# Attention of the later head pairs on 64x64 quadrants, with interleaved tokens, in a fused hourglass attention and ReGLU kernel

## The chip, the cores and the metric

The kernel runs on one core of a Trainium2 chip. The metric is the device time of one execution in microseconds (us); lower is better. The core has a matrix engine (TensorE, PE in the profile, with its weight loads listed as PEld), VectorE (DVE), ScalarE (ACT), GpSimd (POOL) and SyncE (SP), each with an instruction queue of its own that is worked through in order, and DMA queues that are fed from SP, ACT and POOL.

## The reference

The inputs q, k, v have the shape 8 batches x 8 heads x 576 tokens x 64 dimensions, in fp32. Each head has two attentions whose results are added; the outputs of the heads, laid side by side, are 4608 rows of 512, which go through a gated feed-forward network (FFN).

```python
factor = 4; Sd = S // factor; scale = 1.0 / np.sqrt(D)
q_d = q.reshape(B, H, Sd, factor, D).mean(axis=3)     # and k_d, v_d likewise
out_d = sm_attn(q_d, k_d, v_d)                        # full softmax over 144 pooled tokens
out_up = np.repeat(out_d, factor, axis=2)
mask = np.abs(pos[:, None] - pos[None, :]) < factor   # a band of 7 keys
scores = np.where(mask, scale * q @ k.T, -1e9)
out_local = softmax(scores) @ v
x = (out_up + out_local).transpose(0, 2, 1, 3).reshape(B * S, H * D)
out = (np.maximum(x @ w_gate, 0.0) * (x @ w_val)) @ w_out     # d_ff = 1536
```

## The kernel before

**Pairs and chunks.** The 64 (batch, head) problems are handled as 32 head pairs, numbered 0 to 31, four to a batch; the two heads of a pair take 64 of the 128 partitions each. The attention result of a pair is written in fp16 to `xT` (512 features on partitions, 4608 tokens). The FFN runs in 9 chunks of 512 tokens. From chunk 1 on its three products are done by seven-product (Strassen-like) forms, whose matmuls of 128x256 stand at L1200, L1296 and L1037; plain products are L952. While the FFN of one chunk is computed, the attention of four later pairs is woven in.

**Order.** One long string of steps, `SEQ`, sets the order of instructions by hand; a step names a pair (`a` or `b`), a half and a chunk (`scores/a/1@3`). Each engine keeps the order in which its instructions are emitted. For chunks 2 to 6 the same sequence of 242 to 254 steps repeats. Before them lies a front part with the weight loads and pairs 0 to 11, after them the FFN of the last chunks.

**Pairs 0 to 11** use an older method with smaller tiles, whose lines matter here only as examples: scores on 64-row tiles (L622, L633), outputs on 64-column tiles (L723, L732, L744, L753) or full ones (L780, L788), transposes on PE (L550), the mask on DVE (L649), and for pair 11 a pooling of v on POOL (L574, L587).

**Pairs 12 to 31** (`NEW = 12`) use full 128x128 tiles throughout, with both heads in one matmul:

- q and k are cast to fp16 while they are loaded, four DMAs a pair on POOL's queue (L469), and transposed by a DMA of SP (`emit_qkT`, L530), so that dimensions lie on partitions.
- `emit_pool` (L537) sums groups of four tokens of q and k by one DVE reduction.
- `emit_kk` (L800) and `emit_kd` (L807) copy the keys, on ACT, into block-diagonal operands: 64 keys of head 0 in the upper left, 64 of head 1 in the lower right. The zeros around them are filled in beforehand (`emit_zero`, L814, L822).
- `emit_scores` does four matmuls for the pooled scores (L837) and ten for the near ones (L841), in blocks of 58 queries against 64 keys. ACT takes the exponentials (L850, L855), DVE applies the band mask (`emit_mask_st`, L863).
- `emit_out_st` does the denominators with a matrix of ones (L868, L883) and the numerators with v (L868, L888), all on 128 rows and columns. ACT turns the denominators into reciprocals by Ln and Exp; DVE multiplies (`emit_xn_st`, L903) and adds the pooled part, repeated four times, to the near part (`emit_xsum_st`, L907).
- v comes twice: in blocks for L888 (POOL's queue, L487), and in fp32 for its pooled sums (SP's queue, L521). The sums run on POOL: `emit_v2` (L574) and two of `emit_v1` (L582).

**Fences.** Steps called `after`, `tm` and `tn` are tiny copies into a tile `seen` on POOL (L1466, L1525, L1528). They read a result of another engine, so that a buffer's later load on POOL's queue stands behind it. Output rows are stored by SP (`emit_out`, L987). `next` and `sum` steps are the FFN's operand sums on DVE (L1031, L1176); the gate is L1391, and L1314 finishes products.

Of the kernel before, what the change touches and what calls it, by code (L numbers as in the profile page):

```python
# [27 lines left out]
ex/3/0/0 tu/2/1/4 hv/0/0/7 wv/1 hv/0/1/7 tu/2/0/4 ex/3/1/0 vd/3/6 ma/3/0 ones/6 warm/4/1 const/0 const/1 xp/2/1/5  # L28
vc/3/6 xp/2/0/4 ma/3/1 sd/3/6 xe/2/1V/5 xe/2/0A/4 loadq/6 tr/4/0/0 rd/3/6 su/3/4 td/3/6 tr/4/1/2 loadk/6 ru/3/4
hv/1/0/1 ev/4/11A/2 tu/3/0/4 hg/0/0/6 ev/4/10A/2 hg/0/1/6 tu/3/1/4 loadv/6 tr/4/2/3 ev/4/01A/0 ev/4/00A/0 xp/3/1/5  # L30
ev/4/21V/3 ev/4/20V/3 xp/3/0/4 wg/2 hv/0/2/7 xe/3/1V/5 xe/3/0A/4 hg/1/0/0 s1/4/2 wv/2 hv/0/3/7 ex/4/0/2 hv/1/1/1
loadq/7 hg/1/1/0 hg/1/2/0 ed/4/2 ma/4/0 hv/1/2/1 hg/0/2/6 hg/0/3/6 ex/4/1/2 hg/1/3/0 hv/1/3/1 relu/0/6 tr/5/0/2
ma/4/1 tr/5/1/3 loadk/7 relu/1/0 tr/5/2/4 den/4/1/5 ev/5/20V/4 vd/4/6 ev/5/10A/3 hg/3/*/0 ev/5/21V/4 gate/0/7 vc/4/6
# [5 lines left out]
hg/7/*/1 ed/6/4 relu/7/1 ma/6/0 loadv/8 ev/7/11V/0 hg/8/*/2 relu/8/2 hg/6/*/6 relu/6/6 tr/7/2/3 zs/0.1/0@1  # L39
ev/7/21A/3 qk/a2/0@1 qk/b1/0@0 qk/b0/0@0 den/6/1/5 tr/7/0/0 qk/b2/0@0 ev/7/00A/0 zs/0.0/0@1 qk/b3/0@0 qk/a2/1@0  # L40
ev/7/20A/3 ev/7/01V/0 v/b/0@0 den/6/0/4 ln/4 inv hv/8/*/6 hv/6/*/0 gate/8/6 s1/7/4 tr/8/0/2 gate/6/0 ex/7/0/4
ev/8/00A/2 tr/8/1/1 ev/8/10A/1 zs/1.0/0@1 ev/8/01A/2 ev/8/11A/1 ma/7/0 hv/7/*/3 hg/9/*/0 num/6/0/2 v4/a/0@1 ed/7/4
zero/k/0 gate/7/3 ex/7/1/4 relu/9/0 xsum/5 num/6/1/3 xn/2 tr/8/2/4 hv/9/*/1 ev/8/20A/4 qk/a3/1@0 qk/b3/1@0 ma/7/1
ev/8/21A/4 vd/7/7 v/a/1@0 qk/a0/1@0 qk/a1/1@0 hg/10/*/6 den/7/0/4 flip/9 zs/1.1/0@1 qk/a1/0@1 gate/9/1 qk/a3/0@1
v4/b/1@0 den/7/1/5 qk/a0/0@1 xsum/6 wt/0 hv/10/*/3 vc/7/7 relu/10/6 gate/10/3 ln/4 inv num/7/0/6 num/7/1/7 xn/6
next/0/1@0 hg/11/*/2 xsum/7 relu/11/2 zero/b/6 hv/11/*/1 gate/11/1 scores/a/0@1 exp/a1/0@1 wt/1 sumhi/0/0@1 vd/8/0
vc/8/0 ed/a/0@1 p/1/0@1 next/1/1@0 keep/1/0@1 exp/a0/0@1 zero/b/5 p/2/0@1 flip/10 hg/0/0@1 sumhi/1/0@1 p/6/0@1
mask/a1/0@1 o/a01/0@1 qk/b0/0@1 mask/a0/0@1 o/a00/0@1 o/a11/0@1 c11//0@1 p/5/0@1 o/a10/0@1 qk/b2/1@0 wt/2 keep/2/0@1
p/7/0@1 sum/3/0@1 ln/a0/0@1 hv/0/0@1 relu/0/0@1 hg/2/0@1 wt/3 next/0/0@1 keep/3/0@1 p/4/0@1 c22//0@1 gate/0/0@1
next/1/0@1 ln/a1/0@1 inv/a/0@1 xn/a0/0@1 qk/b1/1@0 relu/2/0@1 qk/b3/0@1 zero/b/1 p/3/0@1 xn/a1/0@1 qk/b0/1@0  # L50
qk/b1/0@1 c21//0@1 flip/12 zero/b/0 qk/b2/0@1 c12//0@1 flip/11 pool/b/0@1 next/2/0@1 xsum/a/0@1 vd/10/1 hg/4/0@1
vc/10/1 v/b/1@0 vd/9/5 vc/9/5 hg/1/0@1 relu/1/0@1 hv/1/0@1 gate/1/0@1 v/a/1@1 scores/b/0@1 exp/b0/0@1 mask/b0/0@1
zs/2.0/0@1 hv/2/0@1 exp/b1/0@1 ed/b/0@1 mask/b1/0@1 gate/2/0@1 hg/3/0@1 pool/a/0@1 hv/3/0@1 relu/4/0@1 relu/3/0@1
gate/3/0@1 o/b01/0@1 o/b00/0@1 v2/a/1@1 o/b10/0@1 o/b11/0@1 ln/b0/0@1 zero/v/0 hv/4/0@1 qk/b0/1@1 gate/4/0@1
hg/5/0@1 v/b/1@1 flip/13 zero/d/0 v2/b/0@1 ln/b1/0@1 v4/b/0@1 p/1/1@1 inv/b/0@1 xn/b1/0@1 relu/5/0@1 keep/1/1@1
xn/b0/0@1 hv/5/0@1 hg/0/1@1 gate/5/0@1 xsum/b/0@1 qk/a1/1@1 v1/a/1@1 zero/b/2 relu/0/1@1 p/6/1@1 next/3/0@1
scores/a/1@1 qk/a0/1@1 p/2/1@1 keep/2/1@1 p/7/1@1 qk/a3/1@1 c11//1@1 p/5/1@1 exp/a0/1@1 mask/a0/1@1 exp/a1/1@1
mask/a1/1@1 ed/a/1@1 o/a00/1@1 o/a10/1@1 keep/3/1@1 o/a01/1@1 kk/a1/1@1 qk/a2/1@1 pool/a/1@1 o/a11/1@1 v1/b/1@1
ln/a1/1@1 qk/b3/1@1 hv/0/1@1 ln/a0/1@1 zs/3.1/0@1 p/4/1@1 qk/b1/1@1 c22//1@1 c21//1@1 pool/b/1@1 inv/a/1@1 kd/a0/1@1
p/3/1@1 c12//1@1 qk/a1/0@2 hg/2/1@1 hg/1/1@1 hv/1/1@1 const/2 kk/a0/1@1 kd/a1/1@1 relu/2/1@1 xn/a0/1@1 v/a/0@1  # L60
qk/a2/0@2 v/b/0@1 xn/a1/1@1 scores/b/1@1 flip/14 relu/1/1@1 exp/b0/1@1 hg/3/1@1 zero/v/1 gate/0/1@1 hv/2/1@1
qk/a0/0@2 exp/b1/1@1 gate/1/1@1 mask/b0/1@1 v2/b/1@1 mask/b1/1@1 zero/d/1 zs/2.1/0@1 gate/2/1@1 ed/b/1@1 v4/b/1@1
zs/3.0/0@1 relu/3/1@1 o/b00/1@1 o/b01/1@1 tn/1/0@1 ln/b0/1@1 o/b11/1@1 o/b10/1@1 ln/b1/1@1 inv/b/1@1 hv/3/1@1
qk/b2/1@1 hg/4/1@1 xsum/a/1@1 v/a/0@2 gate/3/1@1 hv/4/1@1 tn/3/0@1 tm/b/1@1 v4/a/1@1 relu/4/1@1 zero/b/3 xn/b1/1@1
xn/b0/1@1 qk/a3/0@2 v/b/0@2 hg/5/1@1 relu/5/1@1 qk/b1/0@2 zero/b/4 gate/4/1@1 xsum/b/1@1 qk/b2/0@2 hv/5/1@1 zero/k/1
qk/b0/0@2 qk/b3/0@2 gate/5/1@1 zero/v/2 xq/0/0@2 v1/a/0@2 up/2.1/0@2 scores/a/0@2 uk/2.1/0@2 v2/b/0@2 sq/4.0.2.1/0@2
sumhi/0/0@2 exp/a0/0@2 xq/1/0@2 next/0/1@1 xq/3/0@2 sumhi/1/0@2 vh/4.6/0@2 sk/4.0.2.1/0@2 up/2.2/0@2 ed/a/0@2
kk/b1/0@2 sq/4.0.2.5/0@2 sq/4.0.2.6/0@2 xq/2/0@2 vh/10.4/0@2 v2/a/0@2 sk/4.0.2.2/0@2 sk/4.0.2.5/0@2 sum/2/0@2
kk/b0/0@2 next/1/1@1 sq/4.0.2.3/0@2 sq/4.0.2.7/0@2 kk/a0/0@2 sf/4.0.2.22/0@2 mask/a0/0@2 sq/4.0.2.2/0@2 up/2.5/0@2
sq/4.0.2.4/0@2 sf/4.0.2.21/0@2 sf/4.0.2.12/0@2 sum/3/0@2 sf/4.0.2.11/0@2 gt/10.4.3/0@2 up/2.6/0@2 uk/2.2/0@2  # L70
pool/b/0@2 gt/4.6.2/0@2 uk/2.5/0@2 sq/0.0.1.1/0@2 sq/0.0.1.5/0@2 sk/0.0.1.5/0@2 sk/0.0.1.1/0@2 o/a00/0@2 o/a01/0@2
ln/a0/0@2 up/2.3/0@2 sq/0.0.1.6/0@2 sk/0.0.1.2/0@2 up/2.7/0@2 uf/2.22/0@2 o/a11/0@2 kd/b0/0@2 sq/0.0.1.7/0@2
sf/0.0.1.22/0@2 kd/b1/0@2 sq/0.0.1.3/0@2 sf/0.0.1.12/0@2 v1/a/1@2 v1/b/0@2 o/a10/0@2 inv/a/0@2 xn/a0/0@2
scores/b/0@2 sq/0.0.1.4/0@2 sf/0.0.1.21/0@2 up/2.4/0@2 sq/0.0.1.2/0@2 pool/a/0@2 uf/2.21/0@2 sf/0.0.1.11/0@2
sq/1.0.0.1/0@2 sq/1.0.0.5/0@2 vh/6.6/0@2 gt/6.6.2/0@2 sk/1.0.0.1/0@2 sq/1.0.0.6/0@2 uf/2.11/0@2 uf/2.12/0@2
sq/1.0.0.2/0@2 vh/0.2/0@2 ed/b/0@2 exp/b0/0@2 v4/b/0@2 o/b00/0@2 sk/1.0.0.5/0@2 sk/1.0.0.2/0@2 mask/b0/0@2
gt/0.2.1/0@2 sq/1.0.0.3/0@2 sq/1.0.0.7/0@2 sf/1.0.0.22/0@2 o/b01/0@2 kk/a1/0@2 sf/1.0.0.12/0@2 kd/a1/0@2 ln/b0/0@2
next/2/0@2 vh/1.3/0@2 kd/a0/0@2 next/0/0@2 sf/1.0.0.11/0@2 sq/1.0.0.4/0@2 sf/1.0.0.21/0@2 gt/1.3.0/0@2
sq/2.2.0.1/1@2 next/1/0@2 v4/a/0@2 sq/2.2.0.5/1@2 sk/2.2.0.5/1@2 scores/a/1@2 pool/b/1@2 vh/7.1/0@2 sk/2.2.0.1/1@2
qk/a1/1@2 o/b11/0@2 ed/a/1@2 gt/7.1.1/0@2 inv/b/0@2 sq/2.2.0.6/1@2 up/0.1/1@2 up/0.5/1@2 qk/a0/1@2 sk/2.2.0.2/1@2  # L80
sq/2.2.0.3/1@2 sq/2.2.0.7/1@2 exp/a0/1@2 qk/a3/1@2 vh/8.5/1@2 sf/2.2.0.12/1@2 o/b10/0@2 v2/b/1@2 kk/b1/1@2
sf/2.2.0.22/1@2 sq/2.2.0.4/1@2 uk/0.1/1@2 after/3/0@2 next/3/0@2 sf/2.2.0.21/1@2 sq/2.2.0.2/1@2 sf/2.2.0.11/1@2
xsum/a/0@2 mask/a0/1@2 up/0.6/1@2 tm/b/0@2 tm/a/1@2 gt/8.5.1/1@2 kd/b1/1@2 uk/0.2/1@2 v/a/1@2 sq/3.2.1.1/1@2
sk/3.2.1.1/1@2 vh/2.4/1@2 xn/b0/0@2 qk/a2/1@2 sq/3.2.1.6/1@2 sq/3.2.1.2/1@2 qk/a1/0@3 qk/b0/1@2 sq/3.2.1.5/1@2
kk/b0/1@2 gt/2.4.0/1@2 v4/b/1@2 sk/3.2.1.2/1@2 up/0.7/1@2 sk/3.2.1.5/1@2 o/a00/1@2 o/a01/1@2 xsum/b/0@2
sq/3.2.1.3/1@2 sq/3.2.1.7/1@2 o/a10/1@2 kd/b0/1@2 uk/0.5/1@2 uf/0.22/1@2 ln/a0/1@2 qk/b1/1@2 up/0.3/1@2 o/a11/1@2
sf/3.2.1.22/1@2 pool/a/1@2 inv/a/1@2 v2/a/1@2 xn/a0/1@2 sq/3.2.1.4/1@2 sf/3.2.1.21/1@2 v/b/1@2 sf/3.2.1.11/1@2
scores/b/1@2 sf/3.2.1.12/1@2 up/0.2/1@2 ed/b/1@2 up/0.4/1@2 exp/b0/1@2 mask/b0/1@2 tm/b/1@2 sq/5.2.1.1/1@2
sq/5.2.1.5/1@2 kd/a1/1@2 v/a/0@3 v4/a/1@2 v1/b/1@2 o/b00/1@2 o/b01/1@2 uf/0.21/1@2 uf/0.11/1@2 uf/0.12/1@2
sk/5.2.1.5/1@2 vh/3.0/1@2 sk/5.2.1.1/1@2 sq/5.2.1.6/1@2 qk/b2/1@2 xsum/a/1@2 gt/3.0.1/1@2 ln/b0/1@2 vh/9.1/1@2  # L90
gt/9.1.2/1@2 qk/a0/0@3 sk/5.2.1.2/1@2 qk/a2/0@3 sq/5.2.1.2/1@2 sq/5.2.1.7/1@2 kk/a1/1@2 kd/a0/1@2 qk/b1/0@3
sf/5.2.1.22/1@2 qk/b3/1@2 inv/b/1@2 o/b11/1@2 sq/5.2.1.3/1@2 sf/5.2.1.12/1@2 sf/5.2.1.11/1@2 o/b10/1@2 xn/b0/1@2
# [187 lines left out]


def _np_stacked():
    r = np.arange(128)
    i, hh = r % 64, r // 64
    q = np.arange(576)
    band = (i[:, None] - q[None, :] % 58 >= 0) & (i[:, None] - q[None, :] % 58 <= 6)
# [24 lines left out]
def kernel(  # L311
# [29 lines left out]
    B0 = 1  # L341
    WK = 112

    NEW = 12
    QB = 58
    NQB = 10

    cst_dr = nc.inline_tensor(_np_constants(), name="cst").ap()
# [1276 lines left out]
```

## Time and profile before

| | |
|---|---|
| median of 3 runs | 346.62 us (346.43 to 347.88) |
| profiled execution | 346.89 us, span 344.9 us |
| granted TensorE clock | 0.998 |
| PE busy | 330.6 us, 96%, 3410 matmuls |
| DVE busy | 294.7 us, 85%, 578 instructions |
| ACT busy | 270.7 us, 78%, 653 instructions |
| POOL busy | 186.5 us, 54%, 268 instructions |
| DMA | 43.91 MB in 162176 packets, mean 127 GB/s |

The span is the time from the first to the last instruction of the profiled execution; its own time contains about 2 us more around it. A group line of the profile reads: line, engine, operation, output <- inputs with their shapes, count | busy us, mean ns of one | idle time of the engine before them, and what ended it. A timeline line reads: start in us, length in us, engine, line, and so on, with the idle time before it in brackets where there was any. A window line gives, for a stretch of time, its length and each engine's busy time with the number of instructions, the granted clock, the DMA share and GB/s.

### The profile page before, as it was taken

Reading aid. Unit: us, or ns where it says so; the run is one execution under the profiler, and the core shown is the slowest. Engines: PE = TensorE matmul, PEld = TensorE weight load, DVE = VectorE, ACT = ScalarE, POOL = GpSimd, SP = SyncE. Lnnn points to the kernel's source line nnn. Section 1 sums busy time; section 2 is a strip of 40 time slices with the busy share of each in tenths; the row PEclk is TensorE's granted clock in tenths of the full one; section 3 lists DMA queues with packets and bytes.
Section 4 is the critical chain, followed back from the end, with each engine's and each line's share of the span. In section 5 each row is a group of like instructions: output and inputs, shape, how many; then the busy total and the mean of one; then the engine's idle time right before and its main releaser. Section 6 shows DMA issues by size and latency. Waiting matters only on the chain.

```text
span 344.9 us, 9106 instructions
## 1 busy us (share of the span) xinstructions
PE 330.6 (96%) x3410; PEld 243.6 (71%) x3410; DVE 294.7 (85%) x578; ACT 270.7 (78%) x653; POOL 186.5 (54%) x268
## 2 busy tenths in 40 slices
PE   8899999998999999999999999999999999999992
PEld 4764555745558786877687868786868588888881
DVE  6694679999999898979998999899899988886971
ACT  4878798976898898887888888988887558787821
POOL 8994645868988489927993899476040000000000
PEclk9999999999999999999999999999999999999999
DMA  9999999999999999999999999999100200011024
GB/s 138 167 171 209 186 194 165 135 159 205 154 171 156 165 132 190 153 167 104 192 149 175 119 196 115 195 121 174 34 33 2 92 2 31 17 64 46 10 68 138
DMA packets 162176, 43.91 MB, mean 127 GB/s; under 512 B 147500, under 2 KB 156820, under 8 KB 162132
## 3 DMA queue, kind: packets, MB, share of 16 engines
q0 software_dynamic: 123136, 19.51, 81.0%
q1 hardware_dynamic: 38884, 23.80, 31.5%
q8 instruction: 26, 0.43, 0.5%
q14 instruction: 18, 0.15, 0.2%
q10 hardware_dynamic: 112, 0.02, 0.1%
HBM read 46.59 MB, written 9.44 MB: 162 GB/s over the span
## 4 chain that ended last, share of the span: by engine, by line
PE 57%; DMA 18%; POOL 10%; DVE 8%; issue 4%; ACT 1%; SPq 1%; ACTq 0%; POOLq 0%; DVEq 0%
PE ps L1296 20%; PE ps L1200 17%; PE ps L952 13%; DMA v<-in_v_dram 5%; DMA wo_sb<-in_moe_w_out_dram 4%; DMA vw<-in_v_dram 4%; DMA wg_sb<-in_moe_w_gate_dram 3%; POOL qk L469 3%; POOL qk L464 3%; POOL vw L514 2%; DVE gT L1391 2%; PE ps L868 2%; PE ps L883 1%; DMA qk<-in_q_dram 1%; PE ps L888 1%
## 5 line engine op out<-in xcount | busy, mean ns | idle before, releaser
L952 PE MATMUL ps<-xT,wv_sb 128*128 128x512 f16 x352 | 90.4, 379 | 0.0
L952 PEld LDWEIGHTS <-wv_sb 128*128 128x128 f16 x352 | 32.6, 98 | 25.6
L1296 PE MATMUL ps<-xT,qk 128*128 128x256 f16 x240 | 41.0, 272 | 0.3 <-DVE xo L1031 0.3
L1391 DVE SCALAR_TENSOR_TENSOR gT<-r,ps 128x512 f16<-128x512 f16 x55 | 37.3, 681 | 3.0 <-PE ps L952 1.4
L469 POOL DMA_DIRECT2D qk<-in_q_dram x46 | 33.7, 738 | 7.7 <-DMA qkT<-qk 4.8
L469 POOL DMA_DIRECT2D qk<-in_k_dram x46 | 33.8, 738 | 6.9 <-DMA wo_sb<-in_moe_w_out_dram 3.3
L1307 ACT COPY ps<-ps 128x256 f32<-128x256 f32 x80 | 29.2, 370 | 7.8 <-PE ps L1296 5.1
L574 POOL TENSOR_TENSOR v<-v 112x384 f32<-112x384 f32 (+1 forms) x21 | 21.1, 1013 | 20.8 <-DMA v<-in_v_dram 20.3
L1296 PE MATMUL ps<-xT,wg_sb 128*128 128x256 f16 x180 | 31.7, 272 | 0.0
L537 DVE TENSOR_REDUCE qkd<-qkT 128x288 f16<-128x1152 f16 x23 | 30.9, 1343 | 0.3 <-ACT r L1312 0.3
L487 POOL DMA_DIRECT2D vw<-in_v_dram x40 | 29.0, 734 | 1.8 <-issue 1.6
L1296 PEld LDWEIGHTS <-qk 128*128 128x128 f16 x240 | 22.2, 97 | 7.9 <-DVE xT L1283 0.7
L1211 ACT COPY ps<-ps 128x256 f32<-128x256 f32 x54 | 19.4, 372 | 10.1 <-PE ps L1200 9.5
L952 PE MATMUL ps<-xT,wg_sb 128*128 128x512 f16 x104 | 26.4, 379 | 0.2 <-DMA wg_sb<-in_moe_w_gate_dram 0.2
L582 POOL TENSOR_TENSOR vd<-v 48x192 f16<-48x192 f32 x40 | 24.3, 607 | 1.9
L1296 PEld LDWEIGHTS <-xo 128*128 128x128 f16 x240 | 22.9, 98 | 3.0 <-DVE xo L1031 0.3
L1312 ACT CAST r<-ps 128x256 f16<-128x256 f32 x55 | 19.2, 374 | 7.2 <-PE ps L1296 5.9
L1296 PE MATMUL ps<-wt,xo 128*128 128x256 f16 x180 | 24.6, 273 | 0.0
L921 ACT ACTIVATE rden<-rden 128x720 f32<-128x720 f32 x28 | 22.5, 803 | 0.5
L1296 PEld LDWEIGHTS <-wg_sb 128*128 128x128 f16 x180 | 16.4, 97 | 5.3
L1296 PEld LDWEIGHTS <-gT 128*128 128x128 f16 x180 | 17.2, 98 | 3.9
L964 DVE TENSOR_TENSOR gT<-r,ps 128x512 f16<-128x512 f16 x24 | 16.1, 679 | 4.3 <-ACT rden L1577 2.2
(181 smaller groups left out, 885.8 us busy)
## 6 DMA issues: line engine op xcount, KB each, us to landing
out_dram<-y_sb SPq DMA_DIRECT2D x24, 256.0 KB, 4.4
v<-in_v_dram SPq DMA_DIRECT2D x20, 192.0 KB, 5.2
qk<-in_k_dram POOLq DMA_DIRECT2D x46, 72.0 KB, 5.0
qk<-in_q_dram POOLq DMA_DIRECT2D x46, 72.0 KB, 4.8
vw<-in_v_dram POOLq DMA_DIRECT2D x38, 80.0 KB, 5.1
v<-in_v_dram SPq DMA_DIRECT2D x20, 144.0 KB, 5.6
out_dram<-y_sb SPq DMA_DIRECT2D x22, 128.0 KB, 1.8
vw<-in_v_dram POOLq DMA_DIRECT2D x12, 168.0 KB, 7.0
```

The costliest lines, as they stand in the source:

```text
L469: nc.gpsimd.dma_start(dst.rearrange("p (j h d) -> p j h d", h=2, d=64)[:, :, hh, :], _dap(src, off + hh * S * D, [[D, 96], [NQ * D, NB], [ ...
L487: nc.gpsimd.dma_start(t[lo : lo + 64, j0:j1, lo : lo + 64], _dap(v, base + j0 * QB * D, [[D, 64], [QB * D, j1 - j0], [1, D]]),)
L537: nc.vector.tensor_reduce(out=qkd[hp % 2].rearrange("p i t -> p (i t)"), in_=qkT[hp % 4][:, 0 : 2 * S].rearrange("p (t f) -> p t f", f=4), ...
L574: nc.gpsimd.tensor_tensor(out=m, in0=t[:, :, 0:128], in1=t[:, :, 128:256], op=ALU.add)
L582: nc.gpsimd.tensor_tensor(out=vp[hp % 3][lo : lo + 48, :, lo : lo + 64], in0=m[:, :, 0:64], in1=m[:, :, 64:128], op=ALU.add)
L921: nc.scalar.activation(out=rden, in_=rden, func=AF.Exp, scale=-1.0)
L952: nc.tensor.matmul(out=out, lhsT=w[:, kk, bass.ts(jj, 128)], rhs=xT[:, kk, c * TCH : (c + 1) * TCH], start=(kk == 0), stop=(kk == 3),)
L1200: nc.tensor.matmul(out=out, lhsT=self.left[i][t], rhs=self.right[i][t], start=(i == 1 and t == 0), stop=(t == n - 1), skip_group_check=True,)
L1211: nc.scalar.copy(out=o, in_=a)
L1296: nc.tensor.matmul(out=out, lhsT=self.left[i - 1][k], rhs=self.right[i - 1][k], start=(i == 1 and k == 0), stop=(k == n - 1), skip_group_c ...
L1307: nc.scalar.copy(out=o, in_=x)
L1391: lambda c, jj, b, t: nc.vector.scalar_tensor_tensor(out=gT[c % 2][:, jj, :], in0=tg[t], scalar=0.0, in1=ps[:, b, :], op0=ALU.max, op1=ALU ...
```

## The change

For pairs 12 to 31:

- **Tokens interleaved.** q and k are loaded with 12 consecutive tokens on each of 48 partitions (instead of 6 blocks of 96), so after the transpose the 48 columns of one block are the tokens w, w+12, w+24 and so on. Adding four neighbouring tokens becomes two additions of whole contiguous blocks (`emit_pool`).
- **64x64 quadrants.** Nothing is block-diagonal any more. `emit_scores` does 8 matmuls for the pooled scores and 24 for the near ones, in blocks of 48 queries against 56 keys; the head selects the row half of the array, the block's parity the column half. `emit_rows` does the denominators and the numerators: there the parity selects the row half and the head the column half; four matmuls of 112 rows x 64 columns come first in each.
- `emit_kk` becomes two ACT copies over 128 partitions, `emit_kd` and its zero fills go, as do the large fills of `zero/b` and `zero/k`.
- `emit_xn_st` is split in three, two of which write runs of four; `emit_xsum_st` then reads and writes contiguous runs. Except for the last batch in the kernel's order (pairs 28 to 31) the tokens stay in the interleaved order in `xT`, and `emit_out` stores the rows of batches 3 to 6 with a stride of 12: 110 store DMAs instead of 50.
- **v pooled on VectorE.** `emit_v2` and `emit_v1` run on DVE, with one instruction each; the fp32 loads on SP are four a pair instead of two.
- **New order.** The first 273 steps stay, but for one dropped `const`; from there on the order is a new one. The fences go, but for two.

Counted in the two programs: PE matmuls 3410 and 4290, with the FFN's unchanged; DVE 580 and 679 instructions; POOL 273 and 192; DMAs issued by SP 121 and 219.

```diff
-    QB = 58
-    NQB = 10
+    QB = 48
+    NQB = 12
+    KB = 56
...
     def emit_load_q1(hp, i):
+        if hp >= NEW:
+            b, off = head_off(hp)
+            t = qksrc[hp % NS].rearrange("p (i j h d) -> p i j h d", i=2, h=2, d=D)
+            nc.gpsimd.dma_start(
+                t[:, i // 2, :, i % 2, :], _dap((q, k)[i // 2], off + i % 2 * S * D, [[12 * D, 48], [D, 12], [1, D]])
+            )
+            return
...
     def emit_pool(hp):
+        if hp >= NEW:
+            x = qkT[hp % 4][:, 0 : 2 * S].rearrange("p (g h x) -> p g h x", g=6, h=2)
+            nc.vector.tensor_tensor(out=half, in0=x[:, :, 0, :], in1=x[:, :, 1, :], op=ALU.add)
+            h = half.rearrange("p g (f t) -> p g f t", f=2)
+            nc.vector.tensor_tensor(
+                out=qkd[hp % 2].rearrange("p i (w t) -> p (i w) t", w=3), in0=h[:, :, 0, :], in1=h[:, :, 1, :], op=ALU.add
+            )
+            return
...
     def emit_scores(hp, p0):
-        for w, o, a, n in ((0, 0, 0, SD), (2, SD, 0, 72), (1, 798, 0, SD), (2, 798 + SD, 72, 72)):
-            nc.tensor.matmul(
-                out=flat[:, lo + o : lo + o + n], lhsT=kd[r2][:, w, :], rhs=qd[:, a : a + n], start=True, stop=True
-            )
...
+        for jj in range(6):
+            for g in range(2):
+                j = 2 * jj + g
+                for hh in range(2):
+                    r = slice(64 * hh, 64 * hh + 64)
+                    at = lo + 224 + 288 * hh + QB * jj
+                    nc.tensor.matmul(
+                        out=flat[64 * g : 64 * g + 64, at : at + QB],
+                        lhsT=kk[r2][r, KB * j : KB * j + 64],
+                        rhs=qt[r, :, 4 * j : 4 * j + 4],
+                        start=True,
+                        stop=True,
+                    )
...
+    def emit_rows(hp, bank, near, far, wide):
...
+        for g in range(2):
+            for hh in range(2):
+                mm(hh, g, 288, 72, far(slice(0, WK), 0, hh), e[0:WK, hh, 72 * g : 72 * g + 72], stop=False)
+        for g in range(2):
+            for hh in range(2):
+                r = slice(64 * g, 64 * g + 48)
+                mm(hh, g, 288, 72, far(r, 1, hh), e[r, hh, SD:], start=False)
+        for jj in range(1 if wide else 6):
+            for g in range(2):
+                for hh in range(2):
+                    r = slice(64 * g, 64 * g + KB)
+                    if wide:
+                        mm(hh, g, 0, 288, near(r, hh, 0), es[hp % 2][r, 288 * hh : 288 * hh + 288])
+                    else:
+                        mm(hh, g, QB * jj, QB, near(r, hh, jj), x[r, hh, jj])
...
-            nc.gpsimd.tensor_tensor(out=m, in0=t[:, :, 0:128], in1=t[:, :, 128:256], op=ALU.add)
+            (nc.vector if hp >= NEW else nc.gpsimd).tensor_tensor(out=m, in0=t[:, :, 0:128], in1=t[:, :, 128:256], op=ALU.add)
...
+            if NEW // NPB <= b < B - 1:
+                real, step, n = real + 12 * (at % 48) + at // 48, 12, 48 - at % 48
```

## The prediction

> **What bounds the kernel now.** I read the page's engine totals first, then the clock, then busy time by stage, and last the waits and the timeline of TensorE (PE).
>
> ```profile
> PE 330.6 (96%) x3410; PEld 243.6 (71%) x3410; DVE 294.7 (85%) x578; ACT 270.7 (78%) x653; POOL 186.5 (54%) x268
> ```
> ```profile
> core 0: us, PE busy (x) PEld busy (x) DVE busy (x) ACT busy (x) POOL busy (x), PEclk, DMA share, GB/s
> 98.91:133.61 34.70, 34.61 (x346) 26.37 (x344) 32.05 (x61) 31.02 (x74) 25.42 (x39) 1.00 1.48 156
> 133.61:169.16 35.55, 34.77 (x347) 26.47 (x345) 31.59 (x59) 30.32 (x72) 27.08 (x41) 1.00 1.32 153
> 169.16:203.80 34.64, 34.39 (x347) 26.43 (x344) 31.27 (x59) 30.32 (x72) 27.14 (x42) 1.00 1.31 164
> 203.80:238.62 34.82, 34.57 (x349) 26.62 (x347) 31.80 (x59) 30.86 (x73) 27.88 (x41) 1.00 1.44 157
> ```
> Each row is one FFN chunk with the attention of four pairs woven in. PE is busy 97 to 100% of it at a granted clock of 1.00, so PE sets the pace; VectorE (DVE) at 89 to 92% is next. The busy time of PE hides how many waits there are, because a matmul's duration includes its pipeline. In a full stream one matmul starts about N/2.4 + 2 ns after another of N columns (in the records 216 ns at 512, 109 at 256, 62 at 144, 28 at 58). By that rule a chunk takes 33.96 us; the four rows average 34.93. So about 0.97 us per chunk, 3.9 us over the four, is waiting, and between 60 and 99 us another 4.5 us or so.
>
> Three prices come from PE's timeline, early in the run, where tiles smaller than 128x128 occur:
>
> ```profile
> 33.88 0.32 PE L744 MATMUL ps<-att,vw 112*64 112x96 f16 x6
> 34.03 0.23 PE L753 MATMUL ps<-att,vd 72*64 72x72 f16 x4
> 34.10 0.27 PE L550 MATMUL ps<-cst_sb,qk 96*64 96x120 f16 x4
> ...
> 35.66 0.23 PE L753 MATMUL ps<-att,vd 72*64 72x72 f16 x4
> 35.82 0.25 PE L622 MATMUL ps<-qkd 64*72 64x144 f16 x2
> ```
> The same four matmuls of L753 are followed after 0.07 us by a group with the same kind of tile (34.03 to 34.10), and after 0.16 us by one of another kind (35.66 to 35.82). Each change of tile size in the trace costs like this: 90 to 97 ns, 59 times. Second, the four L753 matmuls last 230 ns as a group and 196 ns alone (in the groups), so the last starts 34 ns after the first: two 64-column halves of the array run at once. Third, behind a stall a group with 64-column weights starts its first result 24 ns later than usual, one with 128 columns 12 ns.
>
> The other prices, as groups (busy us, mean ns | idle before):
>
> ```profile
> L537 DVE TENSOR_REDUCE qkd<-qkT 128x288 f16<-128x1152 f16 x23 | 30.9, 1343 | 0.3 <-ACT r L1312 0.3
> L903 DVE TENSOR_TENSOR xn<-ps,rden 128x720 f16<-128x720 f32 x20 | 18.0, 901 | 0.1
> L907 DVE TENSOR_TENSOR xT<-xn 128x576 f16<-128x576 f16 x20 | 16.0, 800 | 0.1
> L863 DVE TENSOR_TENSOR att<-att,zero_sb 128x576 f16<-128x576 f16 x20 | 9.5, 473 | 0.0
> L800 ACT COPY kk<-qkT 64x640 f16<-64x640 f16 x20 | 14.4, 722 | 0.3
> L807 ACT COPY cst_sb<-qkd 64x144 f16<-64x144 f16 x40 | 12.4, 309 | 1.0 <-DVE qkd L537 0.6
> L582 POOL TENSOR_TENSOR vd<-v 48x192 f16<-48x192 f32 x40 | 24.3, 607 | 1.9
> L574 POOL TENSOR_TENSOR v<-v 112x384 f32<-112x384 f32 x20 | 19.9, 1004 | 20.8 <-DMA v<-in_v_dram 20.3
> ```
>
> **PE: fewer columns, more changes of tile.** Per new pair, before: pooled scores 432 columns, near scores 576, pooled outputs 864, near denominator 576, near numerator 576: 3024, or 1260 ns, all on full 128x128 tiles. After: 864+1152 score columns on four quadrants at once count 504; twice (denominator, numerator) 4 far matmuls of 72 at two at a time plus 4 of 72 at four count 432; the near ones 576. That is 1512, or 630 ns, if four quadrants run at once. 20 pairs save 20 x 630 = 12.6 us. Against it: a group of four 48-column matmuls streams in 20 ns, but by the 24 ns weight load plus spacing I take 29; 12 groups in each pair x 20 x 7 ns (some overlap taken off) = +1.7. And the tile changes: scores enter and leave 64x64 (2), each output step goes 128x128, 128x64, 64x64, 128x128 (3 each); counted through the program with the neighbours as ordered, changes rise from 59 to 186: 127 x 94 ns = +11.9. The drop in separate groups gives some 0.6 back: **PE +0.4 us**. Bounds: -1.3 without the weight-load term, +12.6 more if quadrants run only two at a time. All of this lies on the path. I take four at a time, since row halves (L622/L633) and column halves (L744/L753) each run side by side in the trace; no row shows both at once.
>
> **DVE.** Before, per pair: 1343+901+473+800 = 3517 ns. After: two fp16 sums, 576 like L863 (473) and 288 between the 576 and the 128-wide rows (300); mask 473; xn in three, 2 x 452 and 302, scaled from the 256-wide PSUM read (L1314, 419); token sum with contiguous runs 473 (800 still in the last four pairs); v sums of 512 fp32 like L1391 (681) and of 256 like L1314 (419). Sum 4025. Five more instructions per pair overlap their neighbours by 75 to 82 ns each, so +0.1 us a pair; with the last four pairs about +4 us over the run. The zero fills of DVE (1 us) go, and so do 3.9 us in which DVE waited at L1031 for a POOL copy that served as a fence. I cost DVE's work at nothing for PE, covered by its 8 to 11% of idle time; without this cover, at most +4.
>
> **The collisions.** POOL's v sums stretch DVE instructions that run beside them:
>
> ```profile
> 72.73 2.06 DVE L649 TENSOR_TENSOR att<-att,cst_sb 112x576 f16<-112x576 f16 x1
> 73.44 1.04 POOL L574 TENSOR_TENSOR v<-v 112x384 f32<-112x384 f32 x1
> 74.86 0.30 PE L780 MATMUL ps<-att,vw 112*128 112x96 f16 x3 [0.80 <-DVE att L649]
> ```
> The mask of L649 has a median of 451 ns; here it took 2060 and PE stood 0.80 us. Ten DVE instructions are stretched, 6.6 us in all, eight beside POOL's v sums. New pairs' v sums leave POOL, so those near 74, 87 and 240 us go, which held PE for 0.97, 0.5 and 0.44: **-1.9 us**. Those of pair 11 (82, 84 us) stay.
>
> **ACT, POOL, queues.** ACT loses 2 x 723 + 2 x 309 = 2064 ns a pair and gains two copies of 128 partitions (estimated 939 from the 640- and 144-wide rows): -22 us; fills, 7.8 us, shrink to about 2. POOL loses 44 us of sums and the 5 us of fence copies, so its q, k and v loads stand behind nothing but their own buffers. SyncE goes from 121 to 219 DMAs: v loads 40 to 80, and output stores 50 to 110 because batches 3 to 6 leave in rows 12 apart; a store takes 0.43 us to issue, +26 us on a queue that also holds the transposes. I cost that at nothing: spread over 180 us it is 15% of SyncE. If a transpose lands late by more than its lead of three pairs, it is paid in full.
>
> **Sum.** With ACT freed by 1.1 us a pair and DVE free of fences, I take a quarter of the 3.9 us of ordinary chunk waits as gone, -1.0 (0 to -3.9). The new order's other moves I put at zero, between -2 and one more wait per chunk (+5). Profiled execution 346.89 us (span 344.9 and 2.0 around it): 346.9 + 0.4 - 1.9 - 1.0 = 344.4; it stands 0.3 above the median 346.62, so **344.1**. A measurement of this kernel can tell about 0.5%, 1.7 us.
>
> **Rivals.**
> *The quadrants take turns (slower).* If the weight loads of the two row halves cannot run together, a group of four takes 2 x 24 = 48 ns whatever its columns: 12 groups x 19 ns and 7 groups of 72 x 16 ns = 340 ns a pair, +6.8 us, 351; if the streams themselves go two at a time, +12.6, 357. It decides once a four-group of 48 columns takes over 35 ns. For it: four loads per 20 ns of stream is four times what any row shows. Against: the pairs in L753 keep a 34 ns spacing with two loads of 64 in it. The Trainium skill, "TensorE: Matmul & The Clock Gate", section LDWEIGHTS, puts a load at columns/1.2, 53 ns for 64 columns, and by that the sum would be some 8 us higher still; the 34 ns spacing speaks against that figure, but no run here shows four loads at once.
> *DVE's queue stops for a v load (slower).* POOL waited 20.3 us in 4 stretches at L574 for these loads, about 5 us each, and nobody minded; now the same wait blocks the evictions PE needs. The collision shows the cover: 1.6 us of stretch cost PE 0.8. One 5 us wait costs PE 4.3; two of them, 352.7. Against: the new order issues the loads earlier than the 5.6 us that one takes to land.
> *The order is tighter (slower).* One more 1 us wait per chunk: 349.
> *More waits vanish (faster).* If the chunk waits mostly go, another -2.2: about 342.
> *The change does nothing to time*: PE stays the bound with the same stream, and only the collisions' 1.9 us move; that is inside my main case.
>
> **Chances.** Main case 0.47 (341.5 to 348; of it 0.31 under 344.9, 0.13 within the bound, 0.03 above), more waits vanish 0.13, turns 0.15, v load 0.12, tighter order 0.13 (0.03 of it within the bound). Faster 0.44, same 0.16, slower 0.40. The range 340.5 to 353.5 leaves out half of the turns case, a third of the v-load case and a third of the fastest, under 0.2. The likeliest case's own range is 341.5 to 348.
>
> **What would show it.** PE's records: near-score groups spaced 29 ns per four if the quadrants run at once, 48 or more if not; 94 ns at each change of tile; PE's chunk stream about 34.0 us as before. No DVE instruction beside a POOL sum over twice its median after 100 us; DVE idle before its v sums near zero (the v-load rival: microseconds, released by DMA). ACT near 245 us, POOL near 135. I am wrong if attention on PE costs over 35 us for the 20 new pairs, or if DVE's idle time in a chunk is ended by DMA.

## The result, and the profile after

The changed kernel takes 383.06 us (median of 3 runs, 381.09 to 383.56) against 346.62: a ratio of 1.1026 (95% interval 1.0953 to 1.1098), 36 us slower, where 344.1 was forecast in a range to 353.5. Its profiled execution has a span of 381.8 us.

The engine totals, and two chunks of the steady part (columns as before: length, busy us of PE, PEld, DVE, ACT, POOL, granted clock, DMA share, GB/s):

```profile
PE 340.5 (89%) x4290; PEld 237.7 (62%) x4290; DVE 302.6 (79%) x677; ACT 284.5 (75%) x599; POOL 136.4 (36%) x187
```
```profile
141.80:182.50 40.70, 35.65 (x532) 24.73 (x520) 32.37 (x79) 33.67 (x65) 17.06 (x24) 1.00 1.62 146
182.50:223.30 40.80, 35.76 (x540) 24.85 (x525) 32.47 (x79) 33.78 (x65) 18.30 (x26) 1.00 1.27 136
```

A chunk takes 40.75 us instead of 34.6 to 35.6, at the same clock. PE is no longer full (88%), DVE is at 80%, and ACT has gone up to 33.7 us a chunk, though it was to lose 4.4 us. From the scores of pair 12 to those of pair 31 it is 200.5 us against 166.8 (33.7 more), and the stretch after that is 81.9 against 79.1. POOL came out at 136 us as forecast; ACT was forecast at 245 and took 284.5. The groups of ACT, and the largest group of PE's FFN products, say why (busy us, mean ns | idle before; the last line is the same PE group in the kernel before):

```profile
L824 ACT COPY att<-qkT 128x576 f16<-128x576 f16 x10 | 26.8, 2685 | 0.0
L824 ACT COPY kk<-qkT 128x576 f16<-128x576 f16 x10 | 26.8, 2678 | 0.6 <-DMA qkT<-qk 0.6
L829 ACT COPY kk<-qkT 128x96 f16<-128x96 f16 x10 | 3.4, 344 | 0.0
L1340 PE MATMUL ps<-xT,qk 128*128 128x256 f16 x240 | 42.5, 276 | 15.6 <-ACT ps L1351 14.8 <-DVE xo L1074 0.8
```
```profile
L1296 PE MATMUL ps<-xT,qk 128*128 128x256 f16 x240 | 41.0, 272 | 0.3 <-DVE xo L1031 0.3
```

L824 is the large key copy of `emit_kk`. It takes 2.68 us, where the prediction had 0.67 (its 939 ns for both copies, less 0.27 for the small one). PE's idle time ahead of this group went from 0.3 to 15.6 us, nearly all of it ended by ACT's copies at L1351. These move a partial product of PE aside, so that PE can go on in its place; below they are called evictions. The timeline shows such a wait behind one copy, and a different chain behind another:

```profile
188.19 2.68 ACT L824 COPY att<-qkT 128x576 f16<-128x576 f16 x1
...
190.39 0.75 ACT L1351 COPY ps<-ps 128x256 f32<-128x256 f32 x1
...
191.19 0.38 PE L1340 MATMUL ps<-xT,qk 128*128 128x256 f16 x2 [1.56 <-ACT ps L1351]
```
```profile
220.31 2.67 ACT L824 COPY kk<-qkT 128x576 f16<-128x576 f16 x1
...
222.51 0.68 ACT L1356 CAST r<-ps 128x256 f16<-128x256 f32 x1
...
223.04 0.38 PE L865 MATMUL ps<-qkT,kk 64*64 64x48 f16 x24 [0.87 <-ACT kk L824]
...
223.23 0.69 DVE L1435 SCALAR_TENSOR_TENSOR gT<-r,ps 128x512 f16<-128x512 f16 x1 [1.08 <-ACT r L1356]
```

In the first, the eviction stands in ACT's queue behind the copy, and PE waits 1.56 us for it. In the second, the scores wait for the keys, the cast L1356 stands behind the copy, and the gate on DVE waits for the cast. Four such copies a chunk make about 6 us (40.75 against 34.8 without them, in e2 below).

The second surprise is the token sum (durations are min/median/max):

```profile
L945 DVE TENSOR_TENSOR xT<-xn x20: 448/452/2730, 122.4 to 309.2; 128x576 f16<-128x576 f16 x20
```

Sixteen take 0.45 us (forecast 0.47). The four of the last batch, which write in the natural token order, take 2.73 us, not 0.8.

What the two slow instructions share is in the diff: they write single fp16 elements 12 elements, that is 24 bytes, apart (`[12, 4]` as the last step of L824's output; `p (t w f) -> p w f t` in L945). Per element both cost the same: 2685/576 = 4.66 ns and 2730/576 = 4.74 ns.

### The profile page after: what moved, and what is told of

Same layout as the page of the kernel before. It is cut to its first block, busy times and chain, and to the rows that moved or that the text cites. A ratio compares the mean times of both kernels' runs of the same rounds, so it can differ in the third digit from the quotient of the medians.

```text
span 381.8 us, 10880 instructions
## 1 busy us (share of the span) xinstructions
PE 340.5 (89%) x4290; PEld 237.7 (62%) x4290; DVE 302.6 (79%) x677; ACT 284.5 (75%) x599; POOL 136.4 (36%) x187
## 3 DMA queue, kind: packets, MB, share of 16 engines
q0 software_dynamic: 128256, 19.69, 79.1%
q1 hardware_dynamic: 45636, 24.74, 34.8%
## 4 chain that ended last, share of the span: by engine, by line
PE 52%; ACT 18%; DMA 15%; DVE 8%; issue 5%; POOL 1%; DVEq 0%; POOLq 0%; ACTq 0%
PE ps L1340 19%; PE ps L1243 15%; PE ps L990 9%; ACT kk L824 6%; ACT att L824 5%; PE ps L894 4%; DMA vw<-in_v_dram 4%; DMA qk<-in_q_dram 3%; DMA wo_sb<-in_moe_w_out_dram 3%; DMA qkT<-qk 3%; DMA v<-in_v_dram 2%; DVE xT L945 2%; DVE gT L1435 1%; ACT ps L1351 1%; PE ps L865 1%
## 5 line engine op out<-in xcount | busy, mean ns | idle before, releaser
L1340 PE MATMUL ps<-xT,qk 128*128 128x256 f16 x240 | 42.5, 276 | 15.6 <-ACT ps L1351 14.8
L498 POOL DMA_DIRECT2D vw<-in_v_dram x40 | 31.8, 807 | 41.8 <-PE ps L894 26.8
L1351 ACT COPY ps<-ps 128x256 f32<-128x256 f32 x80 | 30.7, 394 | 14.4 <-PE ps L1340 12.3
L1435 DVE SCALAR_TENSOR_TENSOR gT<-r,ps 128x512 f16<-128x512 f16 x45 | 30.7, 690 | 7.6 <-ACT r L1356 4.3
L1340 PE MATMUL ps<-xT,wg_sb 128*128 128x256 f16 x180 | 34.8, 276 | 1.8 <-DVE r L1358 1.3
L824 ACT COPY kk<-qkT 128x576 f16<-128x576 f16 x10 | 26.8, 2678 | 0.6 <-DMA qkT<-qk 0.6
L824 ACT COPY att<-qkT 128x576 f16<-128x576 f16 x10 | 26.8, 2685 | 0.0
L935 DVE TENSOR_TENSOR xn<-ps,rden 128x288 f16<-128x288 f32 x40 | 17.7, 454 | 11.3 <-PE ps L894 10.0
L465 POOL DMA_DIRECT2D qk<-in_k_dram x20 | 13.6, 679 | 29.5 <-DMA qkT<-qk 25.8
L1356 ACT CAST r<-ps 128x256 f16<-128x256 f32 x45 | 17.6, 405 | 7.6 <-PE ps L1340 7.1
L1358 DVE TENSOR_TENSOR y_sb<-ps,q 128x256 f32<-128x256 f32 x20 | 8.4, 421 | 12.7 <-ACT y_sb L1356 9.5
```

The source lines that it names most:

```text
L498: nc.gpsimd.dma_start(t[lo : lo + KB, j0:j1], _dap(v, base + j0 * 2 * QB * D, [[D, KB], [2 * QB * D, j1 - j0], [1, D]]))
L824: nc.scalar.copy(out=_sap(o, (0, 128), 4, [[KB, NQB], [1, 12], [12, 4]]), in_=_sap(x, (0, 128), S, [[4, NQB], [48, 12], [1, 4]]),)
L935: nc.vector.tensor_tensor(out=xn_st[:, 0:S].rearrange("p (a j g b) -> p g j a b", a=12, g=2, b=4)[:, i], in0=ps[:, 6 + i, 0:288].rearrange ...
L1340: nc.tensor.matmul(out=out, lhsT=self.left[i - 1][k], rhs=self.right[i - 1][k], start=(i == 1 and k == 0), stop=(k == n - 1), skip_group_c ...
L1351: nc.scalar.copy(out=o, in_=x)
L1356: nc.scalar.copy(out=o, in_=self.d if i == 11 else self.a)
```

## The experiments

Theory W: these spaced writes cost the time, on ACT by standing ahead of the evictions. Rival Q: the quadrants, their tile changes and the many small matmuls. Rival O: the new order. Theory V came up later: DVE's queue stands behind the loads of pooled v. Every time is set against runs of the kernel before on the same chip.

**e1_runs_out.** The key copy walks in another order, with the same result.

```diff
-                out=_sap(o, (0, 128), 4, [[KB, NQB], [1, 12], [12, 4]]),
-                in_=_sap(x, (0, 128), S, [[4, NQB], [48, 12], [1, 4]]),
+                out=_sap(o, (0, 128), 4, [[KB, NQB], [12, 4], [1, 12]]),
+                in_=_sap(x, (0, 128), S, [[4, NQB], [1, 4], [48, 12]]),
```

> The changed kernel with the first key copy of emit_kk (L824) walked in another order: it writes runs of 12 neighbouring keys and reads elements 96 bytes apart, instead of writing elements 24 bytes apart and reading runs of 4. Same elements, same result. Theory W (the spread-out write makes this copy 2.68 us long and blocks ACT's evictions behind it): the copy falls to 0.6 to 0.8 us, a chunk from 40.75 to about 34.7 us, the time to about 348 us (345 to 352). If reads 96 bytes apart cost the same as writes 24 bytes apart: copy 2.7 us and 383 us again. Rival Q (quadrants, changes of tile and the number of small matmuls cost the time): 375 us or more whatever the copy takes. Rival O (the new order is what is slow): likewise 375 or more.

Measured: 360.67 us, ratio 1.0422 (1.0383 to 1.0461), some 22 us less than the changed kernel but above the 345 to 352 expected. The copy fell only to 1.48 us, not to 0.6 to 0.8: reads 96 bytes apart cost 2.56 ns per element, less than spaced writes, but not nothing. A steady chunk takes 36.4 us.

```profile
L824 ACT COPY kk<-qkT 128x576 f16<-128x576 f16 x10 | 14.8, 1475 | 0.0
```

**e2_flat.** The same copy contiguous on both sides.

```diff
+                out=_sap(o, (0, 128), 4, [[KB, NQB], [1, 48]]),
+                in_=_sap(x, (0, 128), S, [[48, NQB], [1, 48]]),
```

> The changed kernel with the first key copy contiguous on both sides, which leaves the keys in the interleaved order (the band then covers other keys: this part of the computation is changed). It is the floor of this copy's price. Theory W: copy about 0.6 us, time 345 to 350 us, within 2 us of the version that writes runs of 12. Rivals Q and O: 375 us or more.

```profile
L824 ACT COPY kk<-qkT 128x576 f16<-128x576 f16 x10 | 6.7, 674 | 1.0 <-DMA qkT<-qk 1.0
```

Measured: 357.16 us, ratio 1.032 (1.0274 to 1.0367). The copy has the forecast price, 0.67 us, and the undisturbed chunks take 34.8 us. One access pattern accounts for some 25 us: the changed kernel stands 36.4 us over the kernel before of its own series, this one 11.4 (357.16 - 345.72). PE's waits for L1351 have nearly gone (0.8 us). An undisturbed chunk is 0.2 us longer than the shortest of the prediction's four rows (34.64), so little is left for rivals Q and O. The time missed the expected 345 to 350, because earlier chunks now take up to 40.6 us. There a new wait shows, which the slow pace had hidden (next).

```profile
151.82 0.69 DVE L600 TENSOR_TENSOR v<-v 112x512 f32<-112x512 f32 x1 [2.75 <-DMA v<-in_v_dram]
...
153.16 1.64 PE L990 MATMUL ps<-xT,wv_sb 128*128 128x512 f16 x4 [2.29 <-DVE gT L1435]
```

DVE stood 2.75 us for a v load before the first sum of pooled v, and PE 2.29 us for the gate behind it. In the changed kernel itself DVE never waited at L600.

**e3_before_slow.** The kernel before, with one of its two key copies writing elements 32 bytes apart, and nothing else of the change.

```diff
-            out=kk[hp % 2][lo : lo + 64, :, lo : lo + 64],
-            in_=_sap(qkT[hp % 4], (lo, 64), S - 3, [[QB, NQB], [1, 64]]),
+            out=kk[...].rearrange("p j (a b) -> p j b a", b=16),              # second head only
+            in_=_sap(qkT[hp % 4], (lo, 64), S - 3, [[QB, NQB], [4, 16], [1, 4]]),
```

> The kernel before, with the key copy of the second head alone written with elements 32 bytes apart (its 64 keys land in another order within a block: this part of the computation is changed; number of elements, partitions and everything else as before). Theory W: this copy goes from 0.72 to about 3.0 us (640 elements at 4.65 ns), ACT gets 45 us more work, and the time rises from 346.6 to 370 to 390 us though nothing else of the change is there. Rivals Q and O: a slow copy on ACT is hidden, 347 to 350 us.

```profile
L800 ACT COPY kk<-qkT x20: 719/1827/2955, 83.2 to 278.2; 64x640 f16<-64x640 f16 x20
```

Measured: 380.39 us, ratio 1.0983 (1.0949 to 1.1018). The second head's copy takes 2.96 us (4.6 ns per element, on 64 partitions as on 128), the steady chunk 42.1 us. The slow copy alone makes the old kernel almost as slow as the changed one, and PE waits in the same place, for the eviction that is L1351 in the changed kernel (14.8 us there) and L1307 here (us in total, times, longest):

```profile
PE ps L1296 <- ACT ps L1307: 15.9, 10, 1.9
```

Q and O are not needed for the bulk of the loss.

**e4_both.** e1, and the last batch's token sums write contiguously and read 96 bytes apart.

```diff
+            out=x.rearrange("p (w f t) -> p w f t", ...) if b < B - 1 else x.rearrange("p (t w f) -> p t w f", ...),
+            in0=xn_st[:, 0:S].rearrange("p (w f t) -> p w f t" if b < B - 1 else "p (w f t) -> p t w f", ...),
```

> As the version with runs of 12 in the key copy, and besides the token sum L945 of the last four pairs writes contiguously and reads elements 96 bytes apart (same result); before, these four wrote elements 24 bytes apart and took 2.73 us against 0.45 for the other sixteen. Theory W, on VectorE too: these four fall to 0.45 to 0.9 us and the time to 2 to 8 us under the version with the key copy alone, about 343 us. If VectorE's reads with stride cost as much, no difference.

```profile
L945 DVE TENSOR_TENSOR xT<-xn x20: 449/452/1428, 117.1 to 281.8; 128x576 f16<-128x576 f16 x20
```

Measured: 355.56 us, ratio 1.027, 5.1 us under e1. The four sums went from 2.77 to 1.43 us each (5.4 us together): nearly all of it is on the path; 3.5 us of it come behind the last pair's scores (82.0 to 78.5 us from there to the end). Two expectations were missed: the sums did not reach 0.45 to 0.9 us, since reads 96 bytes apart have a price too, and the time is not near 343.

**e5_knat and e7_knat_x.** Same result with no spaced write at all: k is loaded in natural order and the key blocks are one contiguous copy.

```diff
-  [[12 * D, 48], [D, 12], [1, D]]
+  [[D, 48], [48 * D, 12], [1, D]] if i // 2 else [[12 * D, 48], [D, 12], [1, D]]      # loads of k
+  out=_sap(kk[hp % 2], (0, 128), 0, [[KB, NQB], [1, KB]]),                            # emit_kk, one copy
+  in_=_sap(qkT[hp % 4], (0, 128), S - 4, [[48, NQB], [1, KB]]),
```

> The changed kernel with all writes 24 bytes apart designed out, same result: k is loaded in natural order (48 consecutive tokens across partitions), so one contiguous copy of 128x672 makes the key blocks and the second key copy goes; k's pooled sums then read every second element (DVE, four sums of 288 and 144 instead of two of 576 and 288); pooled v rows are loaded in natural order too; and the last batch keeps the interleaved token order up to its output stores, so all twenty token sums L945 write contiguous runs (0.45 us), with 12 more strided output rows groups in the tail. Theory W: key copy about 0.75 us, steady chunk 34.8 us as with the flat copy, time 357 less 4 to 5 us of token sums = 352 to 354. What then stays above 346 is of another kind: theory V says it is waits of VectorE's queue for the pooled-v loads in the first chunks (2.75 us at 149 us in the flat run).

> As the first, but the last batch is put back into natural order by the token sum reading 96 bytes apart (1.43 us each for four sums) and its output is stored in whole rows. If the strided stores of the last batch cost time in the tail, this is faster than the first by 1 to 3 us; if they are hidden, it is slower by up to 2 us (4 sums x 1 us on VectorE).

Measured: e5 357.49 us, ratio 1.031 (1.029 to 1.0331); e7 352.32 us, ratio 1.0156 (1.0133 to 1.0179). The copy takes 0.75 us and ACT 244.4 us in all (247.6 in e2, which has the two copies of the prediction's 245). e5 loses its gain in the tail: from the last pair's scores to the end 84.4 us, against 78.2 in e7 and 79.1 before. The last batch's rows, stored 12 apart, are not hidden there: e5 is 5.2 us over e7, where 1 to 3 was expected. With the effects of e2 and e4, 36.4 - 25.0 - 5.1 = 6.3 us over the kernel before would remain; e7 has 5.6. So the two causes add up, as closely as a run can show that also changed the pooled sums and the loads. In e7's waits of DVE:

```profile
DVE v L606 <- DMA v<-in_v_dram: 7.0, 3, 2.7
```

From one pair's scores to those four pairs later it is 34.9 us in e7 where no such wait falls, and 2.5, 2.7 and 2.5 us more in the three stretches with one. That is 7.6 of the 8.7 us by which e7 takes longer than the kernel before between the scores of pairs 12 and 31 (its front and tail are 1.9 us shorter). So the trace puts what is left on these waits; the runs from e8 on try to take them away.

**e6_vpool.** e5 with the v sums back on POOL (`nc.gpsimd` in `emit_v2` and `emit_v1`).

> The same with the pooled-v sums on POOL as in the kernel before (same result). Theory V: VectorE no longer stands behind a v load, the chunks between 97 and 195 us lose 3 to 6 us, and the time is 346 to 350 us. Rival C (collisions of POOL's sums with VectorE, as in the kernel before at 73 us): steady chunks grow by 0.3 to 1 us each and it comes out the same or slower, 352 to 357.

```profile
130.67 2.53 DVE L887 TENSOR_TENSOR att<-att,zero_sb 128x576 f16<-128x576 f16 x1
...
131.58 1.29 POOL L606 TENSOR_TENSOR v<-v 112x512 f32<-112x512 f32 x1
...
133.25 0.32 PE L894 MATMUL ps<-att,ones_sb 56*64 56x288 f16 x4 [0.87 <-DVE att L887]
```

Measured: 361.69 us, ratio 1.0439 (1.0387 to 1.0491), 4.2 us over e5: rival C's outcome, and slower than its 352 to 357. The mask, 0.46 us alone, takes 2.53 beside a POOL sum. Moving the sums to DVE does take the collisions away, and by these two runs the wait for the loads is the smaller evil.

**e8_vlead and e9_tiles.** A first try at an earlier load went too far.

> The changed kernel with k in natural order and the token sums without 24-byte writes (352.3 us), and in the order only three kinds of steps moved per chunk so that pooled-v loads land before VectorE reaches their sum: v4/b/1 about 46 steps earlier (right behind scores/a/0 of the next chunk), v2/a/1 with v1/b/1 about 22 steps later (right ahead of scores/b/1), v2/b/0 about 16 steps later. Theory V (VectorE's queue stands behind these loads: 1.82, 2.67 and 2.47 us of idle time in the run before, each followed by a chunk 2.5 us longer): those three waits go or shrink under 1 us, time 346 to 349 us. If the waits were only where a general lag shows up: still 351 to 353.

> The same as e8_vlead, and the four far matmuls of 112 rows x 64 columns of each output step replaced by two passes over 64x64 quadrants with as many streamed columns (each half of the array then adds its own pooled keys twice and leaves out the other half's: this part of the computation is changed). It takes away one of three changes of tile size per output step, 8 in a chunk. If a change costs 94 ns of the path, as the prediction had it: a steady chunk shrinks by 0.75 us (34.9 to about 34.1), the time by 3 to 4 us. If changes of tile are hidden: no difference over 1 us.

Measured: 391.47 and 391.13 us. The step `v4/b/1` came to lie ahead of the sum that still had to read its buffer, so that sum took the later pair's v (this part of the computation is changed), and had to wait for it:

```profile
DVE vd L609 <- DMA v<-in_v_dram: 37.0, 5, 10.2
```

That is 30 us more of such waits than in e7, and the run is 39 us longer: a wait in DVE's queue reached the end in full and more, since PE's granted clock also fell (0.956 over the run, 0.999 in e7). The question of the tile changes drowned in it.

**e10_v4early and e11_tiles.** The load steps moved only as far as their buffers allow.

> As e7_knat_x (352.3 us; k natural, no write 24 bytes apart, result unchanged), with three of the four pooled-v load steps per chunk moved up to right behind the sum v1 that frees their buffer (21 to 41 steps earlier); nothing else moves. This is what the run with loads ahead of that sum was meant to be: there each sum stood up to 10 us behind the wrong load. Theory V: the waits of VectorE for v loads (7.0 us in 3) fall under 2 us, the three slow stretches of the run before go, and the time is 346 to 349 us. If what holds the loads is not the order but SyncE's queue (stores of 12-row strides and transposes ahead of them): waits stay, 351 to 353 us.

> The same as e10_v4early, and the four far matmuls of 112 rows x 64 columns of each output step replaced by two passes over 64x64 quadrants with as many streamed columns (each half of the array adds its own pooled keys twice and leaves out the other half's: this part of the computation is changed). One of three changes of tile size per output step goes, 8 in a chunk. If a change costs 94 ns of the path: a steady chunk shrinks from about 34.9 to 34.1 us, the time by 3 to 4 us. If changes of tile are hidden: under 1 us.

```profile
DVE v L603 <- DMA v<-in_v_dram: 8.1, 2, 4.6
```

Measured: e10 355.53 us, ratio 1.0264 (1.022 to 1.0308), slower than e7 and outside both expectations: two waits are left, now 4.6 and 3.4 us. The stretches of four pairs with these waits are 5.9 and 4.8 us longer than one without. Where there was none, a chunk looks like this in PE's timeline: the scores of e10's pair at 165.68 and those four pairs later at 200.57, 34.89 us apart.

```profile
165.68 0.27 PE L848 MATMUL ps<-qkd 64*64 64x144 f16 x8
...
200.57 0.27 PE L848 MATMUL ps<-qkd 64*64 64x144 f16 x8
```
```profile
164.46 0.27 PE L848 MATMUL ps<-qkd 64*64 64x144 f16 x8
...
198.60 0.27 PE L848 MATMUL ps<-qkd 64*64 64x144 f16 x8
```

In e11 (the second fence) the same chunk takes 34.14 us, 0.75 us less at the same streamed columns. Changes of tile size are therefore on the path. Counted in the two traces this chunk has nine changes fewer (16 instead of 25), not the eight expected, because two of its output steps follow each other directly; and e11 issues 32 matmuls more in it. So the experiment gives 83 ns a change, net of those matmuls, and that the sum came out at 8 x 94 is partly chance. In total e11 came to 354.24 us, only 1.3 under e10, because its v-load waits grew to 10.7 us.

**e12_v1early.** In each chunk one second sum `v1/a/0` moves up some 50 steps, so that its buffer is free, and the load behind it goes, before the next transpose on SyncE's queue.

> As e10_v4early (result unchanged), and in each chunk the second sum v1/a/0 moved up from behind the scores of the next pair to right behind its first sum v2/b/1, some 50 steps or 14 us earlier, with the load v4/b/1 that needs this buffer right behind it, ahead of the transpose on SyncE's queue. Theory B (the two buffers of pooled v set when a load can start; VectorE then waits for its landing): the remaining waits of 4.6 and 3.4 us go, every chunk takes 34.9 us, and the time is 345.5 to 348 us, level with the kernel before. If SyncE's queue of stores and transposes holds the loads whatever the buffers do: waits of 2 us or more stay and the time is 350 us or more.

```profile
DVE v L603 <- DMA v<-in_v_dram: 3.1, 2, 2.3
```

Measured: 353.21 us (349.39 to 355.08), ratio 1.0187 (1.0128 to 1.0246). In the profiled execution (350.87 us) the two waits of e10 are gone, as theory B has it, though the time is not the 345.5 to 348 that it gave; eleven of the sixteen distances from one pair's scores to those four pairs later are within 1 us of 34.9 us, and a wait of 2.3 us has come up at another pair, whose load had been issued behind four output stores. So both the buffers and SyncE's queue hold these loads; how much each does, run by run, stays open. No run got rid of all these waits, so that the kernel would then be level with the one before is not shown. No version beat the kernel before.

## Why the prediction was wrong

- **ACT's copies, the step that failed.** "Two copies of 128 partitions (estimated 939 from the 640- and 144-wide rows)" measured 2.68 + 0.40 = 3.1 us a pair. The large copy was the term that was mis-sized, 2.68 for 0.67 us; and the sum counted ACT only as relief, although its copies stand in the same queue as the evictions that PE waits for. The price went by the number of elements and overlooked the pattern, which stood in the diff. The trace of before has no write with such a spacing, so the estimate should have had an upper bound far off, and it had none. In place of -22 us, ACT got 13.8 us busier. Some 25 us reached the end (e2), since ACT also evicts PE's results: PE waited 14.8 us for L1351 and 8.9 for the keys. The Trainium skill, "SBUF — State Buffer", section Specifications (TRN2), says that full bandwidth needs at least two accesses to each 16-byte line; 24 bytes apart there is never a second one, and the trace agrees (4.66 ns per element against 674/576 = 1.17 for whole runs). The Trainium skill, "Vector Engine (DVE) Microarchitecture Reference", section 5.2 Measured stream behaviour on trn2 (trn3 not measured), gives, for 32-bit elements, 2.50 ns per element where both sources or the destination step 24 words (96 bytes). e4's reads of 16-bit elements, 96 bytes apart, took 1428/576 = 2.48; the writes 24 bytes apart took 4.7 and are not in its table. Why a write 24 bytes apart costs more than a read 96 bytes apart stays open.
- **The token sum of the last four pairs**, priced at 800 ns, measured 2730; taking 1.34 of its 2.3 us excess away gave 5.1 us (e4).
- **PE, +0.4 us.** Right in kind. In e2 the fastest group of 24 near-score matmuls takes 0.35 us, of which 0.186 is one matmul's own duration: (350-186)/5.75 = 28.5 ns per four. By their starts, the 20 groups of e2 have a median of 31 ns, and e7's lie between 28.5 and 35.3; 29 was taken, and 48 would have meant turns. So four quadrants do run at once, and "the quadrants take turns" is out. The changes of tile size are as many as forecast, 186 in the changed kernel's trace and 59 before; the median extra spacing is 96 ns, with 94 forecast, and e11 shows that they are paid. An undisturbed chunk takes 34.9 us against 34.64 in the shortest row before, which makes some +1.3 over five chunks.
- **DVE.** The sum of 4025 ns a pair measured 453+308+455+2x454+299+452+684+419 = 3978 in sixteen pairs. Right.
- **The collisions.** Right that those of the new pairs go: pair 12's scores begin at 97 to 98 us in the repaired versions (98.9 before), and e6 brings them back at 4.2 us.
- **"A quarter of the chunk waits gone", -1.0.** It rested on a freed ACT, so it fell with the first point; and with ACT freed (e7) an undisturbed chunk is still 34.9 us, so no run shows the gain.
- **The v load in DVE's queue.** The rival was right, but not as the cause here: the slow pace covered it. In the changed kernel DVE never waited for the first of these sums. With the copies mended the trace puts most of what is left on it (7.6 us in e7), and e8, with 30 us more of these waits, ran 39 us longer.

## What to carry to other kernels

Price a copy by the innermost step of both its access patterns, not by its elements: where single 2-byte elements are written 24 or 32 bytes apart it costs four times the write of whole runs (2955 ns against 719), and a re-layout can go into the DMA that loads the data anyway (e7, whose key copy took 0.75 us). On an engine that also evicts PE's results, such a copy can be paid by PE, however idle the engine looks on average (ACT was 75% busy here). And when a change is slower, mend the first cause before ruling out the others: the v-load wait did not exist in the profile until the copies were fast.

## What the runs showed of the hardware

Runs of four fp16 elements cost nothing extra (L935 writes them, 454 ns for 288 elements from PSUM, as forecast). Reads of every second fp16 element cost half as much again (450 ns against 300 for 128x288 in e7). And a standstill of PE of some 2 us can leave it at half its clock for a while, but need not. In e2, behind the wait of 2.29 us shown above, the window reads

```profile
154.60:156.00 1.40, 1.40 (x17) 0.79 (x15) 1.40 (x4) 0.31 (x1) 0.00 (x0) 0.50 1.14 336
158.00:160.00 2.00, 2.00 (x77) 1.60 (x75) 0.86 (x3) 1.54 (x6) 0.00 (x0) 1.00 1.35 103
```

a granted clock of 0.50 that was back at 1.00 within 5 us of the wait's end. In e7 a longer wait at the same place kept the clock at 1.00, and the same four matmuls took 1.02 us instead of 1.64:

```profile
154.07 1.02 PE L990 MATMUL ps<-xT,wv_sb 128*128 128x512 f16 x4 [2.38 <-DVE gT L1435]
```

The clock also fell to about 0.5 behind waits of 1.82 us (the changed kernel, at 290 us), 2.00 (e12), 3.13 and 4.35 (e10). It stayed at 1.00 behind 1.82 (e1, at the same place in the program), 2.10 (e7) and 2.19 (e5). So at about 2 us the length of the wait alone does not decide it, and what does stays open. Where the clock fell, a wait cost more than its own length: in e10 DVE's waits of 4.6 and 3.4 us made their stretches 5.9 and 4.8 us longer.
